# Linear attention fused with two feed-forward layers: when the first layer's weights are converted, and where three mixes stand

## The chip, the cores and the metric

The kernel runs on one core of a Trainium2 chip, as one program. The metric is the time of one execution on the device, in microseconds (us); of several runs the median counts. The core has TensorE (PE: matmuls and transposes, with its weight loads PEld), VectorE (DVE), ScalarE (ACT), GpSimd (POOL) and SyncE (SP, which here only issues DMAs). Matmuls read SBUF and write PSUM, which has eight banks.

## The reference

Three layers run one after the other on 8 batches, 8 heads, 576 positions and heads of 64, in fp32:

```python
def phi(x):                                  # q, k: (8, 8, 576, 64); w_phi: (64, 128)
    proj = x @ w_phi
    proj = proj - np.max(np.abs(proj), axis=-1, keepdims=True)
    return np.concatenate([np.exp(proj), np.exp(-proj)], axis=-1)
q_p, k_p = phi(q), phi(k)
kv = einsum('bhsf,bhsd->bhfd', k_p, v);  z = k_p.sum(axis=2)
x = (q_p @ kv) / (q_p @ z + 1e-6)            # heads laid side by side: (8, 576, 512)

x_prev = x shifted by one position
xk = mu_k * x + (1 - mu_k) * x_prev;  xr = mu_r * x + (1 - mu_r) * x_prev
k = relu(xk @ w_k)                           # w_k: 512 x 1024
x = sigmoid(xr @ w_r) * ((k * k) @ w_v)      # w_r: 512 x 512, w_v: 1024 x 512

h = relu(x @ w_in)                           # w_in: 512 x 1024
c = conv over 3 positions of h, per feature
out = (h * sigmoid(c)) @ w_out               # w_out: 1024 x 512
```

The weights of both feed-forward layers arrive in fp64 and are made fp32 on the chip.

## The kernel before

**Attention, by pairs.** The eight heads of a batch are four pairs, 32 pairs in all, and `block(Pi)` is the TensorE work of one. In the block of pair k TensorE does, from pair 5 on, in this order: the transposes `px` of the result of pair k-1 (whose copy `xT` ScalarE makes); the transposes `pt` of the query features of pair k, which ScalarE turns into `qf` by four Exp, two for each head; the products `pk` of pair k+2 and `pq` of pair k+1, whose maxima `mx` and differences `t` VectorE makes; the sums `pkv` of pair k+1; and the results `pn` of pair k, which VectorE divides into `xn`. In the blocks of pairs 1 to 4 (up to `MS`) `px` stands behind `pk`. `p` is the short last piece of `pk`, and `pr` that of `px` and `pt`. PSUM banks come from two pools: `psa` with five (`pt`, `px`, `pr`, `pkv`, `pn` and some of `pk`), and `psm` with three (the rest of `pk`, `pq`, and all of the layer below). A tile that takes over a bank waits for those who read the bank before: `pkv` takes the one of the second `pt`, and so waits for the last of its `qf`.

**The first feed-forward layer, by units.** `moe(u)` handles half a batch, 16 units in all, in 20 steps: eight `psk` (xk by w_k; ScalarE's Relu makes `kf`, and the square, its cast `kh` and the rest `kl` follow), and twice two `psr` (xr by w_r; Tanh makes `sg`) and two `psv` (by w_v; VectorE makes `x`, which goes to DRAM), each `psv` with two steps. `mix(u, j)` makes xk (j = 0) or xr (j = 1) of unit u from the four `xT` of its batch: for unit 0 four pairs of a ScalarE `mh` and a VectorE `mh`, from unit 1 on four ScalarE `xf` with four VectorE ones, two casts `mh` and two differences `ml`. From unit 1 on a product is three matmuls of hi and lo halves (`mm3`); unit 0 uses the unsplit fp32 weights, one matmul each.

**What runs beside what.** The program counts fifteen places n in a pair; `block(Pi)` is issued at the first. `feed(Pi)` issues the next steps of the units: `SR[Pi]` of them in pairs 4 to 7, ten a pair from pair 8 (`SLOW`). Pairs 0 to 3 have none. `mix(u, 1)` of an odd unit gives the `xT` of a batch back; six are held (`XT`), and a block that would need one more makes the units run on first (`while done[0] * NP <= Pi - 1 - XT`). TensorE's order is the order of the program. The order of the other engines is the scheduler's, which may move an instruction ahead of others.

**The weights' parts.** wk, wr and wv are 20 parts of 512 columns, 512 KB of fp64 each. A part (`step`) is in three pieces: SyncE loads it into one of three buffers `raw`; ScalarE makes `h` from it (the Abs, an ACTIVATE h<-raw); VectorE does two TENSOR_SCALAR and two SCALAR_TENSOR_TENSOR on `h`, after which SyncE writes the 256 KB of `h` to its place in `wkl`, `wrh` or `wvl` and `ready` counts one up. `tick()` issues the load of a new part, the Abs of the one before (through `pre()`, which can also stand earlier) and the end of the one two back. The load of a part needs the buffer of the part three earlier, so VectorE must be through with that. `split` later makes a part's two halves: a cast on ScalarE (`wkh` and the like) and a subtraction on VectorE. From pair 10 on the weights of the last layer pass through in the same way, in smaller pieces `hc` and `whl`.

**When a part is asked for.** The blocks of pairs -1 to 6 call `tick()` twice each. `extras` ticks at the places that `WAT` lists: twice in pair 4, three times in pair 5, four times in pair 6. And `want(n)` ticks at a step of unit 0 or 1 until `n + AHEAD` parts are ready. `split` may run as soon as a part is whole: unit 0 calls it around its `psv`, unit 1 after each `psk` and `psr`.

After the last pair the rest of the units and the second feed-forward layer run (`psh`, `pso`); the change doesn't touch them.

Of the kernel before, what the change touches and what calls it, by code (L numbers as in the profile page):

```python
# [25 lines left out]

NS = 15

MS, SLOW, SR = 4, 8, {4: 6, 5: 6, 6: 7, 7: 9}

WAT = {4: (4, 10), 5: (3, 7, 11), 6: (3, 5, 7, 9)}
DS0 = 10
AHEAD = 2
HS = S // 2
V1 = D + 1

# [6 lines left out]
def fused_kernel(ctx: ExitStack, tc: tile.TileContext, qk, va, wphi, ones2, mu, wk, wv, wr, win, wout, cw, out):  # L43
# [113 lines left out]
    with ExitStack() as p1:  # L157
# [29 lines left out]

        def split(n=None):

            while n is None or cleft[0] < n:  # L190
                if half:
                    hs, ls = half.pop()
                    V.behind("tensor_tensor", ls, f(ls), f(hs), ALU.subtract)
                    cleft[0] += 1
                if whole and (n is None or cleft[0] < n):
                    half.append(whole.pop(0))
                    A.behind("copy", half[0][0], f(half[0][1]))
                if n is None or not half:
                    return
# [3 lines left out]
        def pre():  # L203

            if under and under[0][1] == 2 and not under[0][2]:
                next(under[0][0])
                under[0][2] = True

        def tick():
            pre()  # L210
            new = [wsteps.pop(0), 0, False] if wsteps else None
            if new:
                next(new[0])
            if under and under[0][1] == 2:
                next(under.pop(0)[0], None)
            if new:
                under.append(new)
            for x in under:
                x[1] += 1

        wsteps = [step(wk, wkh, wkl, o) for o in range(0, 4096, 512)]
        for h in range(2):
            for w in ((wr, wrh, wrl), (wv, wvh, wvl)):
                n = w[1].shape[1] // 2
# [163 lines left out]
        def block(Pi):  # L388

            nq, nk = Pi + 1 < B * NP, Pi + 2 < B * NP  # L390
            if 0 <= Pi < B * NP - 3:
                load(Pi + 3)
            if Pi >= 0:
                if Pi > MS:
                    x = column(Pi - 1)
                qf, t1 = turn(Pi)
                pr = psa.tile([P, 512], F32, tag="at", name="pr")
                if Pi > MS:
                    copies = column_end(*x, pr)
                turn_end(qf, t1, pr)  # L400
                if Pi > MS:
                    copies()
            pre()
            if nk:
                tk = front(Pi + 2)
            if -1 <= Pi < 7:
                tick()
            if 1 <= Pi <= MS:
                x = column(Pi - 1)
                column_end(*x, psm.tile([P, 512], F32, tag="mm", name="pr"))()  # L410
            if nq:
                ts[Pi + 1] += centre4(rows4(Pi + 1, 0, "pq"), "tq")
                del xk[Pi + 1]
                sums4(Pi + 1)
            if Pi >= 0:
                results(Pi, qf)
            pre()
            if nk:
                features(Pi + 2, tk)
                if Pi + 2 > 1:  # L420
                    load_v(Pi + 2)
            if -1 <= Pi < 7:
                tick()

        def attention(Pi):
# [30 lines left out]
        def mix_next(u, j):  # L456
            if (u, j) in mixed:
                return True
            if u >= 2 * B or any((u // 2, c) not in xT for c in range(KC)):
                return False  # L460
            mixed[u, j] = mix(u, j)
            if j and u % 2:
                done[0] = u // 2 + 1
            return True

        done = [0]

        def want(n):

            while ready[0] < min(n + AHEAD, 20):  # L470
                tick()
            due[0] += 1

        due = [0]
        needs = [*range(1, 9), 9, 10, 12, 14, 15, 16, 18, 20]

        def moe(u):
            b, hf = divmod(u, 2)

            def mm(ps, wh, wl, xh, xl, first, last):  # L480
                if u:
                    mm3(ps, wh, wl, xh, xl, first, last)
                else:
                    T.matmul(ps, f(wl), xh, start=first, stop=last)

            def need(n):
                want(n)
                if u:
                    split(n)

            def soon():
                if u == 0 and due[0] < len(needs) and ready[0] < min(needs[due[0]] + AHEAD, 20):
                    pre()
            o = hf * HS
            for j in range(2):
                while not mix_next(u, j):
                    yield
            xh, xl = mixed.pop((u, 0))
            k2 = []
            for fp in range(FC // 2):  # L500
                kf = tmps.tile([P, 2, HS], F32, tag="tmp", name="kf")
                for j in range(2):
                    ps = psm.tile([P, 512], F32, tag="mm", name="psk")[:, :HS]
                    fc = 2 * fp + j
                    need(fc + 1)
                    for c in range(KC):
                        w = slice(fc * DM + c * P, fc * DM + c * P + P)
                        mm(ps, wkh[:, w], wkl[:, w], xh[:, c], xl[:, c], c == 0, c == KC - 1)
                    A.activation(kf[:, j], ps, AF.Relu)
                    soon()  # L510
                    if u == 1:
                        split()
                    yield
                if u == 0:
                    kh = main.tile([P, 2, HS], F32, tag="kh", bufs=4, name="kh")
                    A.square(kh, kf)
                    k2.append((kh, kh))
                    continue
                if u == 1:
                    A.square(kf, kf)  # L520
                else:
                    V.tensor_tensor(kf, kf, kf, ALU.mult)
                kh = main.tile([P, 2, HS], F32R, tag="kh", bufs=4, name="kh")
                kl = main.tile([P, 2, HS], F32R, tag="kl", bufs=4, name="kl")
                A.copy(kh, kf)
                V.tensor_tensor(kl, kf, f(kh), ALU.subtract)
                k2.append((kh, kl))
            rh, rl = mixed.pop((u, 1))
            for mp in range(2):
                sg = main.tile([P, 2, HS], F32, tag="sg", bufs=1, name="sg")  # L530
                for j in range(2):
                    ps = psm.tile([P, 512], F32, tag="mm", name="psr")[:, :HS]
                    mc = 2 * mp + j
                    need(9 + 6 * mp + j)
                    for c in range(KC):
                        w = slice(mc * DM + c * P, mc * DM + c * P + P)
                        mm(ps, wrh[:, w], wrl[:, w], rh[:, c], rl[:, c], c == 0, c == KC - 1)
                    A.activation(sg[:, j], ps, AF.Tanh, scale=0.5)
                    soon()
                    if u == 1:  # L540
                        split()
                    yield
                mix_next(u + 1, mp)
                x2 = tmps.tile([P, 2, HS], F32, tag="tmp", name="x2")
                for j in range(2):
                    ps = psm.tile([P, 512], F32, tag="mm", name="psv")[:, :HS]
                    mc = 2 * mp + j
                    need(12 + 6 * mp + 2 * j)
                    for kc in range(FC):
                        w = slice(mc * DFF + kc * P, mc * DFF + kc * P + P)  # L550
                        kh, kl = k2[kc // 2]
                        mm(ps, wvh[:, w], wvl[:, w], kh[:, kc % 2], kl[:, kc % 2], kc == 0, kc == FC - 1)
                    if u < 2:
                        split()
                    soon()
                    yield
                    if u < 2:
                        split()
                    V.scalar_tensor_tensor(x2[:, j], sg[:, j], 1.0, ps, ALU.add, ALU.mult)
                    yield  # L560
                (SY if u else G).dma_start(x2s[b][:, 2 * mp:2 * mp + 2, o:o + HS], x2)
# [12 lines left out]
        load_v(1)  # L574

        def extras(Pi, n):
            if n in WAT.get(Pi, ()):
                tick()
            if n + 1 in WAT.get(Pi, ()):
                pre()  # L580
            if Pi == 7 and n == 14:
                taps()
            if Pi >= DS0 and dsteps and n in (3, 11):
                dsteps[0] = dsteps[0][0](), dsteps[0][1]
            if Pi >= DS0 and dsteps and n in (4, 12):
                raw, step = dsteps.pop(0)
                step(raw)
# [177 lines left out]
```

## Time and profile before

| | |
|---|---|
| median of 3 runs | 1226.19 us (1225.79 to 1226.19) |
| the profiled execution | 1225.83 us, of which its span 1224.0 us |
| PE busy | 1202.0 us (98%), 11920 matmuls |
| PEld busy | 1135.5 us (93%) |
| DVE busy | 762.1 us (62%), 1584 instructions |
| ACT busy | 696.7 us (57%), 1644 instructions |
| POOL busy | 86.3 us (7%) |
| DMA | 100.81 MB, mean 82 GB/s; 223 to 196 GB/s in the first four of the 40 slices, 59 to 80 in the next four |
| chain that ended last | PE 90%, DVE 5%, ACT 2%, issue 1%, DMA 1% |

The span is what the profiler's records cover; the time of the execution is 1.8 us more. Shares of busy time are means over the whole. The first 130 us, in which the weights of the first layer come in and the first pairs run, are where the change is made; after them TensorE is busy in every slice.

### The profile page before, as it was taken

How to read it: one execution, taken by the hardware profiler on the slowest of the kernel's cores; microseconds unless marked ns; L12 is line 12 of the kernel's file. 1: busy time of each engine (PE TensorE's matmuls, PEld its weight loads, DVE VectorE, ACT ScalarE, POOL GpSimd, SP SyncE). 2: the span in 40 equal slices, each digit the busy share in tenths (PEclk: the TensorE clock that was granted, in tenths of full speed). 3: DMA queues.
4: the chain of work that ended last, by engine and by line, in shares of the span. 5: the costliest groups of instructions: out<-in, count | busy, mean ns of one | idle time of the engine just before them, and what ended most of it. 6: DMA issues, size and time to landing. Idle time of an engine off the chain costs nothing.

```text
span 1224.0 us, 29034 instructions
## 1 busy us (share of the span) xinstructions
PE 1202.0 (98%) x11920; PEld 1135.5 (93%) x11920; DVE 762.1 (62%) x1584; ACT 696.7 (57%) x1644; POOL 86.3 (7%) x213
## 2 busy tenths in 40 slices
PE   7899999999999999999999999999999999999998
PEld 6787999999999999999999999998889888888887
DVE  7989676576675765766656534426555754466555
ACT  6777765566565655665555533325654655455554
POOL 1000001111111111111000000000000000000000
PEclk9999999999999999999999999999999999999999
DMA  6665121223232322332110004050122101210220
GB/s 223 221 218 196 59 80 59 86 93 120 89 93 76 117 83 86 93 121 71 50 42 23 11 21 158 20 188 19 44 63 63 43 21 62 63 53 11 63 62 32
DMA packets 56532, 100.81 MB, mean 82 GB/s; under 512 B 10320, under 2 KB 38608, under 8 KB 56400
## 3 DMA queue, kind: packets, MB, share of 16 engines
q1 hardware_dynamic: 40272, 61.65, 14.8%
q0 software_dynamic: 6768, 27.69, 7.4%
q10 hardware_dynamic: 9360, 9.61, 2.8%
q8 instruction: 94, 1.54, 0.5%
q14 instruction: 38, 0.31, 0.1%
HBM read 66.42 MB, written 27.26 MB: 77 GB/s over the span
## 4 chain that ended last, share of the span: by engine, by line
PE 90%; DVE 5%; ACT 2%; issue 1%; DMA 1%; SPq 0%; ACTq 0%; DVEq 0%
PE psh L150 5%; PE psh L152 5%; PE psh L151 5%; PE psv L150 5%; PE pkv L318 5%; PE psv L151 5%; PE psk L151 5%; PE psv L152 5%; PE psk L152 5%; PE psk L150 5%; PE pso L150 5%; PE pso L151 5%; PE pso L152 5%; PE pn L371 4%; PE psr L150 3%; PE psr L151 3%
## 5 line engine op out<-in xcount | busy, mean ns | idle before, releaser
L58 DVE SCALAR_TENSOR_TENSOR ct<-h,cw,ct 128x460 f32<-128x460 f32 (+2 forms) x160 | 111.4, 696 | 84.6 <-ACT ct L58 83.5
L150 PE MATMUL psv<-kh,wvl 128*128 128x288 f32 x480 | 142.2, 297 | 0.0
L151 PE MATMUL psv<-kl,wvh 128*128 128x288 f32 x480 | 141.9, 296 | 0.0
L151 PE MATMUL psk<-ml,wkh 128*128 128x288 f32 x480 | 141.7, 295 | 0.0
L152 PE MATMUL psk<-mh,wkh 128*128 128x288 f32 x480 | 141.4, 295 | 0.0
L152 PE MATMUL psv<-kh,wvh 128*128 128x288 f32 x480 | 141.1, 294 | 0.0
L150 PE MATMUL psk<-mh,wkl 128*128 128x288 f32 x480 | 140.9, 294 | 0.0
L152 PE MATMUL psh<-xh,wih 128*128 128x462 f32 (+1 forms) x320 | 118.9, 372 | 0.0
L151 PE MATMUL psh<-xl,wih 128*128 128x462 f32 (+1 forms) x320 | 118.8, 372 | 0.0
L151 PE MATMUL pso<-gl,woh 128*128 128x460 f32 (+1 forms) x320 | 117.9, 370 | 0.0
L152 PE MATMUL pso<-gh,woh 128*128 128x460 f32 (+1 forms) x320 | 117.7, 370 | 0.0
L58 ACT ACTIVATE kf<-psk 128x288 f32<-128x288 f32 x128 | 52.2, 408 | 111.5 <-PE psk L152 105.6
L150 PE MATMUL psh<-xh,wil 128*128 128x462 f32 (+1 forms) x320 | 107.3, 372 | 0.0
L58 ACT ACTIVATE h<-psh 128x462 f32<-128x462 f32 (+3 forms) x128 | 47.8, 409 | 76.8 <-PE psh L152 75.6
L150 PEld LDWEIGHTS psv<-kh,wvl 128*128 128x128 f32 x480 | 90.3, 188 | 0.8
L151 PEld LDWEIGHTS psv<-kl,wvh 128*128 128x128 f32 x480 | 90.4, 188 | 0.0
L150 PEld LDWEIGHTS psk<-mh,wkl 128*128 128x128 f32 x480 | 90.2, 188 | 0.1
L151 PEld LDWEIGHTS psk<-ml,wkh 128*128 128x128 f32 x480 | 90.2, 188 | 0.0
L152 PEld LDWEIGHTS psv<-kh,wvh 128*128 128x128 f32 x480 | 90.2, 188 | 0.0
L152 PEld LDWEIGHTS psk<-mh,wkh 128*128 128x128 f32 x480 | 90.2, 188 | 0.0
L58 ACT ACTIVATE kp<-t 128x512 f32<-128x512 f32 x128 | 70.3, 618 | 34.6 <-PE pkv L318 28.9
L58 DVE SCALAR_TENSOR_TENSOR x<-sg,psv 128x288 f32<-128x288 f32 x64 | 29.0, 454 | 97.5 <-PE psv L152 91.4
(108 smaller groups left out, 2822.7 us busy)
## 6 DMA issues: line engine op xcount, KB each, us to landing
rqk<-qk POOLq DMA_DIRECT2D x29, 576.0 KB, 4.8
va<-va POOLq DMA_DIRECT2D x30, 325.0 KB, 4.8
x2s<-x SPq DMA_DIRECT2D x30, 288.0 KB, 2.3
raw<-wk SPq DMA_DIRECT2D x8, 512.0 KB, 5.4
raw<-wv SPq DMA_DIRECT2D x8, 512.0 KB, 4.0
raw<-win SPq DMA_DIRECT2D x16, 256.0 KB, 2.9
raw<-wout SPq DMA_DIRECT2D x16, 256.0 KB, 2.9
x2r<-x2s ACTq DMA_DIRECT2D x16, 231.0 KB, 2.6
```

The costliest lines, as they stand in the source:

```text
L58: x = op(*a, **k)
L150: T.matmul(ps, wl, xh, start=first, stop=False)
L151: T.matmul(ps, wh, xl, start=False, stop=False)
L152: T.matmul(ps, wh, xh, start=False, stop=last)
L318: T.matmul(o[r:r + 64], k_[:, r:r + 64], v_, start=(i == 0), stop=(i == len(prods) - 1))
L371: T.matmul(pn[b_][64 * r:64 * r + 64, j], qf[h_][:, c, o:o + 64], kv[:, c, h_], start=(j == 0 and c == 0), stop=(j == 4 - b_ and c == 1))
```

## The change

- **Parts.** In the blocks of pairs -1 to 4 the first `tick()` stays, and the second only in pair -1's. So pairs 0 to 3 issue one part instead of two, pair 4 one, and the blocks of pairs 5 and 6 none. The table `WAT`, its ticks in `extras` and `AHEAD` go. Instead every step of unit 0 that needs a part ticks until `ready` has reached the larger of what it needs and `PRE + RATE * (at + 1)`, with `at` the number of the step: one part a step, six ahead. `soon()` issues the Abs of a part that the next step will ask for.
- **Splits.** A `split` without a number does nothing until all 20 parts are ready.
- **Mixes.** Units 0 and 1 start with `mix(u, 0)` alone. `mix(0, 1)` is called after the fourth `psk` of unit 0, `mix(1, 1)` after the second of unit 1 (before: in unit 0, between its last `psr` and `psv`), and `mix(1, 0)` after the last `psr` of unit 0 (before: after its second `psr`).
- **Steps.** `SR[7]` goes from 9 to 6.

```diff
-MS, SLOW, SR = 4, 8, {4: 6, 5: 6, 6: 7, 7: 9}
-WAT = {4: (4, 10), 5: (3, 7, 11), 6: (3, 5, 7, 9)}
-AHEAD = 2
+MS, SLOW, SR = 4, 8, {4: 6, 5: 6, 6: 7, 7: 6}
+PRE, RATE = 6, 1.0
@@ split
         def split(n=None):
+            if n is None and ready[0] < 20:
+                return
@@ block
-            if -1 <= Pi < 7:
+            if -1 <= Pi <= MS:
                 tick()
...
-            if -1 <= Pi < 7:
+            if Pi == -1:
                 tick()
@@ want
-        def want(n):
-            while ready[0] < min(n + AHEAD, 20):
-                tick()
-            due[0] += 1
-        due = [0]
-        needs = [*range(1, 9), 9, 10, 12, 14, 15, 16, 18, 20]
+        needs = [*zip([*range(11), 12, 14, 15, 16, 18], [*range(1, 11), 12, 14, 15, 16, 18, 20])]
+        def goal():
+            at, n = needs[0]
+            return min(20, max(n, int(PRE + RATE * (at + 1))))
+        def want():
+            while ready[0] < goal():
+                tick()
+            needs.pop(0)
@@ moe
             def need(n):
-                want(n)
                 if u:
                     split(n)
+                else:
+                    want()
             def soon():
-                if u == 0 and due[0] < len(needs) and ready[0] < min(needs[due[0]] + AHEAD, 20):
+                if u == 0 and needs and ready[0] < goal():
                     pre()
-            for j in range(2):
+            for j in range(2 if u > 1 else 1):
                 while not mix_next(u, j):
                     yield
...
+                if fp == 1 - u:
+                    mix_next(u, 1)
...
-                mix_next(u + 1, mp)
+                if u:
+                    mix_next(u + 1, mp)
+                elif mp:
+                    mix_next(1, 0)
@@ extras
-            if n in WAT.get(Pi, ()):
-                tick()
-            if n + 1 in WAT.get(Pi, ()):
-                pre()
```

How this moves instructions shows at three places. The first is VectorE at the start of pair 3's block: the last division `xn` of pair 2, and what stands up to the differences `t` of `pk`. Before:

```order
L58 TENSOR_SCALAR xn<-pn,rd 128x128
L58 TENSOR_SCALAR h<-h 128x512
L58 TENSOR_REDUCE mx<-p_876 128x1
L58 TENSOR_REDUCE mx<-p_877 128x1
L58 TENSOR_SCALAR h<-h 128x512
L58 TENSOR_TENSOR t<-p_876,mx 128x128
L58 TENSOR_TENSOR t<-p_877,mx 128x128
L58 SCALAR_TENSOR_TENSOR h<-raw,h 128x512
L58 TENSOR_REDUCE mx<-pk 128x4 x2
L58 SCALAR_TENSOR_TENSOR h<-raw,h 128x512
```

After:

```order
L57 TENSOR_SCALAR xn<-pn,rd 128x128
L57 TENSOR_REDUCE mx<-p_849 128x1
L57 TENSOR_REDUCE mx<-p_850 128x1
L57 TENSOR_TENSOR t<-p_849,mx 128x128
L57 TENSOR_TENSOR t<-p_850,mx 128x128
L57 TENSOR_REDUCE mx<-pk 128x4 x2
L57 TENSOR_TENSOR t<-pk,mx 128x512 x2
L57 TENSOR_SCALAR h<-h 128x512
```

The four instructions of one part, which stood among the small steps and around the reduction of `pk`, are gone from there; the pair's remaining part follows behind `t`.

The second is ScalarE at the end of pair 4, among the `kf` of unit 0, and at the start of pair 5's block, which begins with the copy `xT`. Before:

```order
L58 ACTIVATE kf<-psk 128x288
L58 ACTIVATE h<-raw 128x512
L58 ACTIVATE kf<-psk 128x288
L58 ACTIVATE kh<-kf 128x576
L58 ACTIVATE kf<-psk 128x288 x2
L58 COPY xT<-px 128x512
L58 ACTIVATE kh<-kf 128x576
L58 ACTIVATE qf<-pt 128x512 x4
```

After:

```order
L57 ACTIVATE kf<-psk 128x288 x2
L57 ACTIVATE kh<-kf 128x576
L57 ACTIVATE h<-raw 128x512
L57 ACTIVATE kf<-psk 128x288
L57 ACTIVATE h<-raw 128x512
L57 ACTIVATE kf<-psk 128x288
L57 COPY xT<-px 128x512
L57 ACTIVATE kh<-kf 128x576
L57 ACTIVATE qf<-pt 128x512 x3
L57 ACTIVATE h<-raw 128x512
L57 ACTIVATE qf<-pt 128x512
```

An Abs now stands ahead of each of the last two `kf` of pair 4 (the latter part 10's), and part 11's ahead of the fourth `qf`.

The third is ScalarE at pair 12's block, one of the later pairs, with the last `kf` of pair 11 ahead of it. Before:

```order
L58 ACTIVATE kf<-psk 128x288 x2
L58 ACTIVATE hc<-raw 128x256
L58 COPY xT<-px 128x512
L58 ACTIVATE qf<-pt 128x512 x4
L58 CAST kh<-kf 128x576
L58 ACTIVATE qf<-pr 128x64 x4
L58 COPY xT<-pr 64x64 x2
L58 CAST whl<-hc 128x256
L58 ACTIVATE xf<-xT,mu_76 128x288 x4
```

After:

```order
L57 ACTIVATE kf<-psk 128x288
L57 CAST kh<-kf 128x576
L57 ACTIVATE sg<-psr 128x288
L57 COPY xT<-px 128x512
L57 ACTIVATE qf<-pt 128x512 x2
L57 CAST whl<-hc 128x256
L57 ACTIVATE xf<-xT,mu_76 128x288 x2
L57 ACTIVATE qf<-pt 128x512 x2
L57 ACTIVATE qf<-pr 128x64 x4
```

The cast `whl` and two of the `xf`, which stood behind the block's `qf`, stand between its second and third, and a unit's step more is done ahead of the block (the `sg` is the first of its `psr`).

## Rows read from the trace of the kernel before

**Rows 1.** Windows: stretch, length, busy us (count) by engine, clock, DMA share, GB/s

```profile
47.20:58.88 11.68, 9.49 (x196) 8.44 (x196) 11.61 (x29) 9.24 (x25) 1.07 (x2) 1.00 0.66 213
69.53:135.98 66.45, 65.09 (x749) 55.01 (x745) 57.82 (x127) 43.84 (x107) 5.10 (x12) 1.00 0.56 189
135.98:148.79 12.81, 12.81 (x100) 12.81 (x97) 7.13 (x14) 11.43 (x25) 0.00 (x0) 1.00 0.05 18
200.00:500.00 300.00, 300.00 (x3941) 295.45 (x3941) 204.01 (x471) 182.66 (x474) 45.62 (x62) 1.00 0.31 95
```

**Rows 2.** Waits of TensorE, whole span: who for whom, total us, times, longest

```profile
PE psv L484 <- DVE x L58: 0.7, 1, 0.7
...
PE pn L371 <- DVE t L58: 0.7, 1, 0.7
```

**Rows 3.** Order of time, TensorE: start, us, operation, form, count, [idle before <-releaser]

```profile
50.33 1.25 PE L261 MATMUL pk<-wp,rqk 64*128 64x128 f32 x16 [1.24 <-DVE xn L58]
51.51 0.66 PE L330 MATMUL px<-ident,xn 128*128 128x128 f32 x4
...
69.53 11.91 PE L484 MATMUL psk<-mh,wkl 128*128 128x288 f32 x48
```

**Rows 4.** Order of time, VectorE in pair 3's block

```profile
50.35 0.42 DVE L58 TENSOR_SCALAR h<-h 128x512 f32<-128x512 f32 x1
50.69 0.48 DVE L58 TENSOR_REDUCE mx<-p 128x1 f32<-128x128 f32 x2
...
51.81 0.69 DVE L58 SCALAR_TENSOR_TENSOR h<-raw,h 128x512 uint32<-128x512 uint32 x1
52.41 1.29 DVE L58 TENSOR_REDUCE mx<-pk 128x4 f32<-128x512 f32 x2
```

**Rows 5.** Order of time, TensorE and VectorE in pair 5's block

```profile
84.23 1.06 PE L261 MATMUL pq<-wp,rqk 64*128 64x128 f32 x16
84.42 1.29 DVE L58 TENSOR_REDUCE mx<-pk 128x4 f32<-128x512 f32 x2
```

**Rows 6.** Order of time, SyncE's DMA issues and ScalarE in pair 4

```profile
72.45 0.47 SPq L184 DMA_DIRECT2D wrh<-h  x1
73.02 0.90 SPq L174 DMA_DIRECT2D raw<-wv  x1
...
77.05 0.68 ACT L58 ACTIVATE h<-raw 128x512 f32<-128x512 f32 x1 [0.97 <-DMA raw<-wv]
```

**Rows 7.** Tile raw, 60 to 81 us: its loads, issue to landing

```profile
DMA to landing us min/median/max: 3.7/4.7/5.6
```

**Rows 8.** Order of time, TensorE and ScalarE in pair 8's block

```profile
148.79 0.60 PE L330 MATMUL px<-ident,xn 128*128 128x128 f32 x4
...
153.71 2.09 PE L318 MATMUL pkv<-va,kp 128*64 128x65 f32 x64
...
151.01 0.57 ACT L58 COPY xT<-px 128x512 f32<-128x512 f32 x1
```

**Rows 9.** Order of time, TensorE and ScalarE in pair 10's block

```profile
198.71 0.60 PE L330 MATMUL px<-ident,xn 128*128 128x128 f32 x4
...
202.64 1.56 PE L318 MATMUL pkv<-va,kp 128*64 128x65 f32 x46
...
200.84 0.68 ACT L58 CAST kh<-kf 128x576 fp32r<-128x576 f32 x1
201.41 1.11 ACT L58 ACTIVATE qf<-pt 128x512 f32<-128x512 f32 x2
```

**Rows 10.** Order of time, ScalarE behind pair 12's `qf`

```profile
252.33 0.41 ACT L58 CAST whl<-hc 128x256 fp32r<-128x256 f32 x1
252.64 1.87 ACT L58 ACTIVATE xf<-xT,mu 128x288 f32<-128x288 f32 x4
```

**Rows 11.** Order of time, ScalarE and TensorE in pair 26's block

```profile
592.91 2.05 ACT L58 ACTIVATE qf<-pt 128x512 f32<-128x512 f32 x4
594.04 1.16 PE L261 MATMUL pq<-wp,rqk 64*128 64x128 f32 x16 [0.67 <-ACT qf L58]
```

## The prediction

> **What bounds the kernel now.** I read first the busy time by stretch, then TensorE's waits, then the order of time around each wait. From 200 to 500 us TensorE is busy for all of 300.00 us while VectorE has 204 and ScalarE 183 [rows 1]: there TensorE sets the time, and whatever it is made to wait comes on top in full. The first pairs are another regime: pair 3's block takes 11.68 us, VectorE works 11.61 of them and TensorE 9.49 [rows 1]; it is VectorE's. Between them, from 69.53 to 135.98 us, both are nearly full (65.09 and 57.82 of 66.45), with waits of 0.7 for t and 0.7 for x [rows 1, 2]. So the change can gain in pairs 0 to 4 and has to pay where it puts the work. All matmuls stay, so only waits count.
>
> **Two parts a pair become one (pairs 0 to 3).** A part costs VectorE two TENSOR_SCALAR, each 0.34 from its start to the next instruction's (50.35 to 50.69), and two SCALAR_TENSOR_TENSOR at 0.60 (51.81 to 52.41): 1.88 us [rows 4]. A pair loses one part. Not all of it is gained, since the part's steps filled VectorE's wait for pk. The matmuls pk start at 50.33, when xn is done, and take 1.18 until px at 51.51 [rows 3]; VectorE's reduction stands 0.19 behind their end (84.42 behind 84.23) [rows 5], so it can start at 51.70. Without the fillers VectorE is free at 50.35 plus twice 0.40 for the four small steps, 51.15: it idles 0.55. Net 1.33 a pair. Pairs 1 to 3 stand ahead of the first psk, so that moves from 69.53 [rows 3] to 65.5: **4.0 gained** so far. Nothing else is late there: ScalarE loses an Abs too.
>
> **The parts arrive in pairs 4 to 6.** Five parts more (9.4 us) have to go through VectorE there, where it had 66.45 - 57.82 = 8.6 idle [rows 1]; one split of 0.6 leaves. That alone fills it. What I expect to hurt first is ScalarE, whose queue now holds the Abs of the coming parts between the kf and ahead of the copy xT, so that a late load holds everything behind it. There are three raw buffers: part 10's load waits until part 7 is done, and part 7's until part 4 is. In the trace the write that marks the end of pair 4's part leaves at 72.45, the next load 0.57 later, and it has landed at 77.05, 4.03 after its issue [rows 6]. Now, with 4 x 1.33 less: part 4 done at 67.1, load 67.7, landed 71.7, Abs 0.6, VectorE 1.88, so part 7 is done at 74.3; load 74.9, landed 78.9. Behind it on ScalarE stand Abs (0.6), the sixth kf (0.35) and the copy xT, at 79.9. TensorE's px comes after six psk (11.91 with the last one's tail [rows 3], 11.8 to the next start) at 77.3. In pair 8 of the trace, the one block where that copy was late, pkv followed 2.70 behind the copy's start (151.01 to 153.71) [rows 8]; with kh and part 11's Abs put among the qf (1.2 more) pkv is at 83.8 instead of px + 3.93 = 81.2 [rows 9]. **Pair 5 waits 2.6.** By the same steps (part 11 done 89.2, load of 14 landed 93.8, done 96.4, load of 17 landed 101.0, Abs) pair 6's copy starts at 101.6 to 102.9 against a px at 99.9 to 100.5: pkv 0.5 to 1.2 late, **0.9** taken.
>
> The Trainium skill's page "DMA: Bandwidth & Descriptors" (Anatomy of one DMA) gives 2.0 us and bytes over 436 GB/s, an estimate of 3.2 us for 512 KB; by it both loads together come 1.7 earlier and the sum below would be 1228.8. The rows speak against it: 3.7 is the shortest load of 60 to 81 us, the median is 4.7 [rows 7]. The same page (Issuing engines are not separate DMA queues) says that transfers of all issuers interleave on the same 16 engines, which bears on the third rival.
>
> **The mixes.** Of mix (0,1) nothing moves: the order shows its steps still in pairs 1 to 4, so 0. Mix (1,1) goes from pair 6 to unit 1's first steps, where ScalarE already had 11.43 of 12.81 us [rows 1], and three psk now stand ahead of pair 7. Behind the first kf ScalarE has three kf (0.31), three casts of weights (0.51), four xf (0.43), one mh and one square (0.57 each): 5.3 us, while TensorE reaches px 3.2 behind the first psk. The copy starts 2.4 behind px, another mh of 0.57 stands ahead of the qf, and pkv is at px + 2.4 + 0.57 + 2.70 = px + 5.7: **pair 7 waits 1.8**, where it waited for nothing. Pair 8: pkv was 4.92 behind px (148.79 to 153.71) [rows 8], so 1.0 late; now sg, a square and an mh stand around the copy, by the same count px + 5.2: 1.2 late.
>
> The waits of pairs 5 to 8 are then 2.6 + 0.9 + 1.8 + 1.2 = 6.5; before they were 0.7 + 0.7 + 1.0 = 2.4 [rows 2, 8]. With the 4.0 gained the stage is at **+0.1**: the relief is given back. Splits that come later cost nothing: ScalarE's and VectorE's share of them is in the counts above.
>
> **Every second pair from 12 to 26.** With pair 7's rate at 6 and four forced steps the units run one step later against the pairs, and the scheduler puts other ScalarE work into the blocks. In pair 12 and seven like it the cast whl and two xf now stand between the second and third qf; pkv takes over the bank that the fourth qf reads, so it waits for that. The nearest row is pair 10, with a kh of 0.57 in that place (200.84 to 201.41): its qf end at 201.41 + 0.96 = 202.37, pkv starts at 202.64 [rows 9]. From the end of a qf to the matmul that waits for it is 0.17 (592.91 + 0.96 to 594.04) [rows 11]; so pair 10 had 0.10 to spare. Now 0.31 + 2 x 0.43 = 1.17 [rows 10] stands where 0.57 stood: 0.60 more, and the copy starts about 0.02 later, so pkv waits **0.52**. TensorE has no slack there [rows 1]: 8 x 0.52 = 4.2. Pairs 10 and 28 are changed alike by smaller pieces, 0.35 each by the same count; the 0.67 in pair 26 [rows 11] goes: **+4.2** together. Bounds: without the 0.17 it is 0.35 a pair, and 0.67 is the largest wait of this kind in the trace, so +2.1 to +5.4.
>
> **Sum.** The profiled execution: 1225.83 + 0.1 + 4.2 = 1230.1. The median of the runs is 0.36 above that execution: **1230.5**, 0.35% slower.
>
> **Rivals.**
> *The relief survives.* ScalarE is never the last to release TensorE in pairs 5, 6 and the later ones: then 4.0 and 2.4 are gained, pairs 7 and 8 cost 3.0, and the time is 1222.8. It decides at ScalarE's copies: part 10's load would have to be in at 77 rather than 78.9, and the fourth qf in pair 12 half a microsecond sooner. For it: VectorE, not ScalarE, was the engine with no idle time. Against: two loads in a chain, none shorter than 3.7.
> *Even.* The stage gives the relief back, but in pairs 12 to 26 pkv does not wait: 1226.3. It needs the fourth qf released at px + 3.93; the count has it at px + 4.45. For it: kh in the same place cost nothing in pair 10. That the change does not do what it says in one piece (mix (0,1)) is in all of these.
> *The loads collide.* 768 KB a part, read and written back, at one in some 2.4 us. If both loads of the chain take 5.6, the longest there [rows 7], and not 4.03, pair 5 waits 3.1 longer: 1233.6, and more if pair 6's do too. For it: the DMA share is already 0.56 there [rows 1] with fewer parts.
>
> **How the numbers follow.** Forecast 0.5, even 0.2, relief 0.15, collision 0.15. The forecast's own range is 1227.9 to 1232.5, by the bounds of +2.1 to +5.4 and of 0.5 to 1.2 in pair 6. About 0.2%, 2.5 us, is what a measurement of this kernel can tell from no change. Slower by more: 0.46 of the forecast's 0.5 and the collision, 0.61; within: 0.04 and the even case, 0.24; faster: 0.15. The range 1224.5 to 1234.0 leaves out most of the relief (below it) and the worse half of the collision (above).
>
> **What would show it.** Right: first psk near 65.5; pair 2's and 3's blocks 10.35 apart; in pair 5 TensorE waits for xT or qf, with ScalarE's Abs waiting for raw just before; in pairs 12, 14 and so on to 26 pkv waits for qf by about half a microsecond. Wrong: blocks of 9.8 (the pk wait is not there), pair 5 of 8.5, or no wait of TensorE for ScalarE from pair 12 on. The prediction falls if psv waits for a part's write, which I put at nothing, or if blocks that I did not count wait.

## The result: 0.55% slower

The changed kernel takes 1233.49 us (median of 6 runs, 1230.43 to 1234.03), the kernel before, beside it, 1225.97 (1225.27 to 1226.19): a ratio of 1.0055, with a 95% interval of 1.0043 to 1.0067. The forecast was 1230.5, in a range of 1224.5 to 1234.0. The sign came out as forecast, and so did the waits that make it; the terms of pairs 5 and 6 were too small by 3.7 us together, since the parts that they hang on came later than worked out. The profiled execution took 1233.2, with a span of 1231.4 (before: 1225.83 and 1224.0). From the page of the profile after:

```profile
span 1231.4 us, 29055 instructions
PE 1205.6 (98%) x11920; PEld 1138.4 (92%) x11920; DVE 768.4 (62%) x1584; ACT 697.5 (57%) x1644; POOL 82.5 (7%) x213
PE 87%; DVE 6%; ACT 5%; DMA 1%; issue 1%; ACTq 0%; SPq 0%; DVEq 0%
```

The matmuls are the same 11920. What is new is in the chain that ended last (the third line): ScalarE has 5% of it, 2% before. TensorE's waits over the whole span, in the manner of [rows 2], name it: the copy xT ahead of pk, and qf ahead of pkv eleven times.

```profile
PE pk L262 <- ACT xT L57: 5.4, 3, 2.6
PE pkv L319 <- ACT qf L57: 4.7, 11, 0.5
...
PE pk L262 <- DVE xn L57: 4.1, 4, 1.2
```

Where the 7.4 us of span went is seen by holding the length of each pair's block on TensorE (from px to the first step of a unit behind pn) against before:

| | before | after | difference | forecast |
|---|---|---|---|---|
| first psk starts at | 69.53 | 65.44 | -4.1 | -4.0 |
| pair 5 | 8.50 | 12.67 | +4.2 | +2.6 |
| pair 6, with the wait of psv behind it | 9.37 + 0.70 | 11.65 | +1.6 | -0.5 |
| pair 7 | 8.49 | 10.22 | +1.7 | +1.8 |
| pair 8 | 9.48 | 9.61 | +0.1 | +0.2 |
| pairs 9 to 28 | 20 x 8.50 + 1.0 | 20 x 8.50 + 5.08 | +4.1 | +4.2 |
| sum | | | +7.6 | +4.3 |

(The forecast's pair 6 is 0.9 less 0.7 and 0.7.) From pair 29 on the blocks are alike. TensorE's last matmul ends 7.8 later, and what follows it is 0.4 shorter. In pair 12's block the order of time has ScalarE as the order of instructions said, with the cast and two xf between the second and third qf, and TensorE's pkv waiting for the fourth:

```profile
254.60 1.10 ACT L57 ACTIVATE qf<-pt 128x512 f32<-128x512 f32 x2
255.57 0.43 ACT L57 CAST whl<-hc 128x256 fp32r<-128x256 f32 x1
255.86 0.99 ACT L57 ACTIVATE xf<-xT,mu 128x288 f32<-128x288 f32 x2
256.73 1.10 ACT L57 ACTIVATE qf<-pt 128x512 f32<-128x512 f32 x2
...
257.88 2.09 PE L319 MATMUL pkv<-va,kp 128*64 128x65 f32 x64 [0.46 <-ACT qf L57]
```

Such blocks are 9.03 for 8.50: 0.53, where the forecast, from the 0.10 that pair 10 had to spare [rows 9], had 0.52.

Pairs 5 and 6 are where the forecast fell short. In pair 5, ScalarE first (the Abs of parts 9, 10 and 11, the copy and the fourth qf), then TensorE:

```profile
77.15 0.67 ACT L57 ACTIVATE h<-raw 128x512 f32<-128x512 f32 x1 [1.22 <-DMA raw<-wr]
77.72 0.40 ACT L57 ACTIVATE kf<-psk 128x288 f32<-128x288 f32 x1
80.40 0.66 ACT L57 ACTIVATE h<-raw 128x512 f32<-128x512 f32 x1 [2.27 <-DVE h L57]
80.96 0.40 ACT L57 ACTIVATE kf<-psk 128x288 f32<-128x288 f32 x1
81.25 0.58 ACT L57 COPY xT<-px 128x512 f32<-128x512 f32 x1
...
83.74 0.70 ACT L57 ACTIVATE h<-raw 128x512 f32<-128x512 f32 x1
84.29 0.63 ACT L57 ACTIVATE qf<-pt 128x512 f32<-128x512 f32 x1
...
79.24 0.38 PE L262 MATMUL pk<-wp,rqk 64*128 64x128 f32 x2
81.89 1.85 PE L262 MATMUL pk<-wp,rqk 64*128 64x128 f32 x13 [2.27 <-ACT xT L57]
...
85.29 2.09 PE L319 MATMUL pkv<-va,kp 128*64 128x65 f32 x64
```

Part 10's Abs stands in the queue ahead of the last kf and the copy, as forecast, and it starts at 80.40, where 78.9 was forecast. Its load was issued at 75.62 and took 4.7. (The profile puts the wait down to VectorE, which had finished part 9 at 80.20; in the program this Abs waits for two DMAs alone, its load and an older write of h.) The copy comes at 81.25, and the second of pk's two banks, which px had, is free only then: TensorE stands still in pk already, after two of its sixteen matmuls.

Behind this wait the clock falls. The windows of the stretch (columns as in [rows 1]) have TensorE still from 79.60 to 81.89, and then at half its clock:

```profile
79.60:81.89 2.29, 0.02 (x1) 0.00 (x1) 1.36 (x3) 1.49 (x4) 0.00 (x0) 0.91 0.90 322
81.89:83.90 2.01, 2.01 (x17) 2.01 (x19) 1.98 (x7) 2.01 (x5) 0.00 (x0) 0.50 0.94 282
83.90:85.30 1.40, 1.40 (x19) 1.28 (x16) 1.40 (x5) 1.40 (x7) 0.00 (x0) 0.64 0.54 199
...
104.00:106.62 2.62, 0.04 (x2) 0.01 (x1) 2.58 (x7) 2.62 (x7) 0.00 (x0) 1.00 0.83 265
106.62:109.00 2.38, 2.38 (x40) 2.25 (x42) 2.38 (x8) 2.38 (x9) 0.00 (x0) 1.00 0.30 111
```

A granted clock of 0.50 is 1.2 GHz, the lower of its two levels; with the mean of 0.64 in the third row, TensorE worked at it for some 3.0 us behind the wait. That costs little here, since pkv has to wait for the fourth qf in any case. The kernel of e3 (below) is the same up to pair 7, and in its trace the clock is 1.00 throughout pair 5:

```profile
79.91 0.58 ACT L57 COPY xT<-px 128x512 f32<-128x512 f32 x1
...
80.53 1.16 PE L262 MATMUL pk<-wp,rqk 64*128 64x128 f32 x14 [0.91 <-ACT xT L57]
82.09 1.16 PE L262 MATMUL pq<-wp,rqk 64*128 64x128 f32 x16 [0.40 <-ACT qf L57]
83.63 2.09 PE L319 MATMUL pkv<-va,kp 128*64 128x65 f32 x64 [0.38 <-ACT qf L57]
```

From the copy's start to pkv it is 3.72 there and 4.04 here, so the clock makes 0.3 of the 4.2. What else sets the two traces apart is when the copy comes: 79.91 there, where part 10's load was issued at 75.02 and took 3.9, and 81.25 here. The block of e3 is 11.00, 2.5 over 8.50.

In pair 6 the copy comes at 106.00, behind the Abs of parts 16 and 17 and four xf of mix (1,0):

```profile
103.17 0.67 ACT L57 ACTIVATE h<-raw 128x512 f32<-128x512 f32 x1 [2.75 <-DMA raw<-wv]
103.74 1.79 ACT L57 ACTIVATE xf<-xT,mu 128x288 f32<-128x288 f32 x4
105.45 0.65 ACT L57 ACTIVATE h<-raw 128x512 f32<-128x512 f32 x1
106.00 0.56 ACT L57 COPY xT<-px 128x512 f32<-128x512 f32 x1
...
99.53 0.54 SPq L173 DMA_DIRECT2D raw<-wv  x1
DMA to landing us min/median/max: 5.5/5.5/5.5
```

The last two lines are part 17's load: issued at 99.53, in at 105.0. TensorE stood still for 2.58 in this block, longer than in pair 5, and its clock stayed at 1.00 (the last two of the windows). Where the clock fell in pair 6 (e1, e3 and e5 to e8), the stretch from the copy to the end of the block is 8.7 to 8.8; without a fall (here, e4 and e9) it is 7.2. So a fall costs some 1.5 there, and 0.3 in pair 5 here.

The six runs of the changed kernel differ with the clock too: the one whose mean granted clock was 1.000 took 1230.43, the two with 0.999 took 1231.0 and 1233.2, the three with 0.996 to 0.998 took 1233.77 to 1234.03. How much of that is the clock, and how much the late loads that go before a fall, these runs don't show. The kernel before, which has no wait over 0.7 there [rows 2], varies by 0.9.

### The profile page after: what moved, and what is told of

Same layout as the page of the kernel before. It is cut to its first block, busy times and chain, and to the rows that moved or that the text cites. A ratio compares the mean times of both kernels' runs of the same rounds, so it can differ in the third digit from the quotient of the medians.

```text
span 1231.4 us, 29055 instructions
## 1 busy us (share of the span) xinstructions
PE 1205.6 (98%) x11920; PEld 1138.4 (92%) x11920; DVE 768.4 (62%) x1584; ACT 697.5 (57%) x1644; POOL 82.5 (7%) x213
## 3 DMA queue, kind: packets, MB, share of 16 engines
q10 hardware_dynamic: 9360, 9.61, 2.8%
## 4 chain that ended last, share of the span: by engine, by line
PE 87%; DVE 6%; ACT 5%; DMA 1%; issue 1%; ACTq 0%; SPq 0%; DVEq 0%
PE psh L149 5%; PE psh L151 5%; PE psh L150 5%; PE pkv L319 5%; PE psv L150 5%; PE psv L151 5%; PE psv L149 5%; PE psk L149 5%; PE pso L149 5%; PE psk L150 5%; PE psk L151 5%; PE pso L150 5%; PE pso L151 5%; PE pn L372 4%; PE psr L149 3%; PE psr L150 2%
## 5 line engine op out<-in xcount | busy, mean ns | idle before, releaser
L149 PE MATMUL pso<-gh,wol 128*128 128x460 f32 (+1 forms) x320 | 88.0, 371 | 0.3 <-ACT gh L57 0.3
```

Of the source, the lines that this page charges most:

```text
L149: T.matmul(ps, wl, xh, start=first, stop=False)
```

## The experiments

Times of the experiments are medians beside runs of the kernel before on the same chip: 1225.74 for e1 to e4, 1225.82 for e5 to e8, 1225.64 for e9 to e12.

**The two halves of the change, apart (e1, e2).** e1 is the changed kernel with the mixes and SR[7] of before:

```diff
-MS, SLOW, SR = 4, 8, {4: 6, 5: 6, 6: 7, 7: 6}
+MS, SLOW, SR = 4, 8, {4: 6, 5: 6, 6: 7, 7: 9}
...
-            for j in range(2 if u > 1 else 1):
+            for j in range(2):
...
-                if fp == 1 - u:
-                    mix_next(u, 1)
...
-                if u:
-                    mix_next(u + 1, mp)
-                elif mp:
-                    mix_next(1, 0)
+                mix_next(u + 1, mp)
```

> The changed kernel with the mixes where they stood before and 9 steps again in pair 7; the parts stay as changed. Theory (three separate prices: the parts gain 4.1 in pairs 1 to 3 and cost 4.2 + 2.3 - 0.7 in pairs 5 and 6 through ScalarE's copy xT; mixes and steps cost 1.7 in pair 7 and 4.1 in pairs 10 to 28): blocks of pairs 5 and 6 stay long (12.7 and 11.6), pair 7 is back at 8.5 and every second pair from 12 on at 8.5; 1226.0 - 4.1 + 4.2 + 2.3 - 0.7 = 1227.7 (1225.5 if TensorE's clock does not fall in pair 5). Rival (the mixes, not the parts, hold up pairs 5 and 6): 1222.

e2 is the kernel before with these edits the other way round.

> The kernel before with only the three mixes moved and 6 steps in pair 7; the parts and splits stay as before. Theory: first psk at 69.5, pairs 5 and 6 as before (8.5 and 9.4), pair 7's block 1.7 longer, pairs 10, 12 to 26 and 28 about 0.5 longer each: 1226.0 + 1.7 + 0.1 + 4.1 = 1231.9. Rival (the mixes hurt only where the parts are late): 1226.

e1 took 1227.67 (ratio 1.0016, 1.0007 to 1.0025): pairs 5 and 6 at 11.06 and 13.04, pair 7 at 8.50, pairs 9 to 28 at 1.03 over 20 x 8.50, as before. e2 took 1230.50 (1.0040, 1.0028 to 1.0053): pair 5 at 8.50, pair 7 at 10.23, pairs 9 to 28 at 5.08 over. Of the 1.4 that it is under the expected time, 1.0 is that pair 6 and the psv behind it wait less than before (8.50 and 0.54 for 9.37 and 0.70). So the two halves come near the whole: 1.9 for the parts, 4.8 for mixes and steps, 6.7 of 7.5, and each cost shows in the pairs that it was put down to. The rival that the mixes hold up pairs 5 and 6 is out.

**One step (e3).** In the changed kernel, pair 7 gets 5 steps:

```diff
-MS, SLOW, SR = 4, 8, {4: 6, 5: 6, 6: 7, 7: 6}
+MS, SLOW, SR = 4, 8, {4: 6, 5: 6, 6: 7, 7: 5}
```

> The changed kernel with 5 steps in pair 7 for 6, which puts the units back by one step against the pairs. Theory (the waits of pkv for qf in every second pair from 10 on come from that one step alone): they go, blocks of 8.5 from pair 9 on with pair 26's 9.46 back; 1233.5 - 4.1 = 1229.4, pairs 1 to 8 unchanged. Rival (they come from where mixes and splits stand): 1233.5.

It took 1228.25 (1.0017, 1.0008 to 1.0026). Pairs 9 to 28 are back at 1.02 over 20 x 8.50, so the 4.1 there come from the one step by which the units ran on against the pairs, and from nothing else in the change. The other 1.1 is not located: pairs 5 and 6 take 11.00 and 13.65 in this trace, 12.67 and 11.65 in the change's, and the eleven runs go from 1225.83 to 1230.78.

**Parts four ahead instead of six (e4).**

```diff
-PRE, RATE = 6, 1.0
+PRE, RATE = 4, 1.0
```

> The changed kernel with PRE 4 for 6: the last Abs ahead of pair 5's copy xT is that of part 9, not 10, and ahead of pair 6's that of part 15, not 17. Theory (the copy stands behind an Abs whose load has not landed): part 9 was in at 77.1, so the copy comes at 78.3, TensorE does not wait in pair 5 (8.5 to 9.2 for 12.67) and its clock does not fall; pair 6 keeps the four xf ahead of the copy and waits 1 to 2; psk and psr do not wait for parts: 1228 to 1230. Rival (the loads collide, whatever stands in ScalarE's queue): 1233.5 or more, with TensorE waiting for parts.

It took 1235.33 (1.0077, 1.0065 to 1.0090): 1.8 slower than the change, where 3.5 to 5.5 faster was expected. The first half of the theory held: the copy came at 77.97, and pairs 5 and 6 took 9.59 and 9.34. But TensorE now waited for the parts themselves:

```profile
PE psv L489 <- DMA wvl<-h: 3.3, 4, 1.6
PE psr L489 <- DMA wrh<-h: 2.4, 1, 2.4
```

So the wait does not go with the copy's place behind the Abs: taken out of ScalarE's queue, it turns up where a part is needed. (With PRE 4 each part is also asked for two steps later, so a share of it can be of this edit's own making.)

**Half loads, half VectorE work (e5, e9).** e5 loads 256 columns of a part and reads them twice; e9 lets VectorE's four instructions cover 256 columns.

```diff
 # e5
-            SY.dma_start(raw, src[:, o_])
+            SY.dma_start(raw[:, :256], src[:, o:o + 256])
...
-            high, low, hu = raw[:, :, 1], raw[:, :, 0], h.bitcast(U32)
+            high, low = [raw[:, :256, i].unsqueeze(1).to_broadcast([P, 2, 256]) for i in (1, 0)]
...
 # e9, ahead of VectorE's four instructions
+            h, hu, low, high = h[:, :256], hu[:, :256], low[:, :256], high[:, :256]
```

> The changed kernel with loads of half a part (256 columns, 256 KB for 512 KB; the Abs and VectorE's steps keep their size and read those columns twice, so half of the first layer's weights are left out and their values are wrong). Theory (the copy xT of pairs 5 and 6 stands behind an Abs whose load is still under way): loads of 2.5 to 3 for 4.4, the chain of three buffers some 1.5 a part shorter, no wait of ScalarE for raw ahead of these copies: blocks of 8.5 to 9.5 in pairs 5 and 6 for 12.67 and 11.65, TensorE's clock stays; pairs 12 to 26 keep their 9.03; 1227 to 1228. Rival (VectorE, full in pairs 4 to 6, is what holds the parts): both blocks stay over 11 and the time over 1232.

> The changed kernel with whole loads, but VectorE's four instructions of a part on 256 of its 512 columns (half of the first layer's weights stay unconverted, their values are wrong). Theory after e5 (VectorE is the engine that sets when a part is done: 2.25 a part when it does parts one after the other, and with half loads it had no idle left ahead of pair 6's copy): a part takes 1.2, pairs 1 to 3 lose another 0.3 each, pairs 5 and 6 take 8.5 to 9.5 for 12.67 and 11.65; 1225 to 1227. Rival (the loads are the limit, 4.3 each through three buffers): pairs 5 and 6 stay at 11 or more; 1231 or more.

e5: 1230.67 (1.0043, 1.0029 to 1.0057); e9: 1233.42 (1.0069, 1.0053 to 1.0084). Neither theory stands alone. With loads of 2.9 (median) for 4.3, pairs 5 and 6 still took 10.51 and 12.73: VectorE then went from part to part without a gap and was still late. With half of VectorE's work they took 13.67 and 10.59, ScalarE standing for loads of 4.5; in e9 the order also has part 11's Abs, not part 10's, as the last ahead of pair 5's copy. One window per kernel, from pair 1's px to the end of the last part on VectorE, shows both (before, after, e5, e9, in this order, each from its own trace):

```profile
28.16:121.36 93.20, 85.30 (x1276) 73.46 (x1276) 88.59 (x203) 68.63 (x170) 7.56 (x17) 1.00 0.63 211
```

```profile
28.43:123.35 94.92, 87.19 (x1279) 76.00 (x1279) 88.04 (x197) 65.85 (x164) 8.64 (x13) 0.98 0.64 204
```

```profile
27.79:119.82 92.03, 85.71 (x1271) 74.66 (x1271) 88.24 (x197) 65.82 (x164) 8.51 (x13) 0.98 0.49 161
```

```profile
27.43:119.05 91.62, 85.28 (x1266) 74.21 (x1266) 74.88 (x197) 65.64 (x166) 7.23 (x13) 0.98 0.63 208
```

The third figure with a count is VectorE. Its work up to the last part is the same 88 us whichever pairs the parts stand in, and before it had only 4.6 of 93.2 idle. So the last part could end at most 4.6 sooner even if VectorE never stood still: that bounds what moving parts can gain. It is not the only limit. In the changed kernel VectorE stood still for 6.9 of 94.9. In e9, with 13 less for VectorE, the last part ends only 4.3 sooner (119.05 for 123.35), and with half loads 3.5 sooner. And in both the changed kernel and e9 part 17 is in by 105.0 and 102.3, but VectorE takes it up only at 116.91 and 114.50, behind pair 6's own steps. Which limit sets the last part in which order is not shown.

**A part back in pairs 0 and 1 (e6, e7, e8).** All three are e1 with a second tick again, e7 and e8 also with PRE 5:

```diff
             if Pi == -1:      # e6, e7: Pi < 1;  e8: Pi < 2
                 tick()
```

> e1 with a second part in pair 0 again (pair 0's block did not get shorter by losing it: 11.16 before, 11.43 after). The order puts part 11's Abs, not part 10's, ahead of pair 5's copy. Theory: 0 to 0.3 lost in pair 0; pair 5 gains little (the chain of loads is one part ahead, and the copy waits for one part more): 11; pair 6, behind part 16 as in e1, gains one part's 2.3: 10.7; 1225.4. Rival (the position counts, not the part): 1227.7, or more with one part more through VectorE.

> e6 with PRE 5, so that pair 5's copy stands behind part 10 and pair 6's behind part 15, each with its load one part earlier than in e1. Theory: pair 5 8.7 to 9.2, pair 6 9 to 9.5 (four xf still ahead of its copy), psr and psv wait 0 to 2 for parts that come later; pairs from 7 on as in e1: 1224. Rival (what the blocks gain is waited for by psr and psv, as in e4): 1227 or more.

> e7 with a second part in pair 1 as well: 1.4 of the 4.1 given back there, and all loads from pair 4 on one part earlier again. Theory: pairs 5 and 6 8.5 to 9, nothing waits for a part in the steps: 1224 to 1225. If e7 is already free of these waits, this is 1.4 slower than e7.

They took 1228.91, 1228.17 and 1229.83 (1.0027, 1.0021 and 1.0038): all three theories missed, by 3.5, 4.2 and 4.8 or more, and the rivals of e6 and e7 came. In e6 pair 5 took 13.14, with part 11's Abs ahead of its copy. In e7 pair 5 took 8.90 as expected, but pair 6 took 12.39, and psv waited 1.7 for wvl; e8 has the same waits and pays 1.8 more ahead of the first psk (67.91 for 66.12).

**The kernel before with one or two parts fewer (e10, e11).**

```diff
-            if -1 <= Pi < 7:                            # the second tick of a block
+            if -1 <= Pi < 7 and Pi != 3:                # e10
...
+            if -1 <= Pi < 7 and Pi not in (2, 3):       # e11
```

> The kernel before without the second part in pair 3 (nothing else). Theory (a part in pairs 1 to 3 costs 1.46 there and 2.25 of VectorE later, where before has 8.6 idle in pairs 4 to 6): first psk 1.46 earlier; one part fits into the idle time, pairs 5 and 6 lose 0 to 1: 1225.0 (1224.3 to 1226). Rival (each part moved costs TensorE what it gains, or more): 1226 to 1227.

> The kernel before without the second part in pairs 2 and 3 (nothing else). Theory: first psk 2.9 earlier; 4.5 more for VectorE in pairs 4 to 6, of 8.6 idle: waits of 1 to 2 in pairs 5 and 6 or in psr and psv; 1224.5 to 1225.5. Rival (each part moved costs what it gains or more): 1226.5 to 1228.

They took 1227.49 (1.0018, 1.0009 to 1.0027) and 1232.62 (1.0058, 1.0045 to 1.0070): the rival was right, and for two parts the cost was higher than it said. In e10 the part left out shortened no block (px of pair 4's block 11.68 behind that of pair 3's, as before), and the last psv of unit 0 waited for a part's write, and then ran at the lower clock, 5.81 for 4.04:

```profile
120.00 4.15 PE L484 MATMUL psv<-kh,wvl 128*128 128x288 f32 x16 [0.71 <-DVE x L58]
126.18 5.81 PE L484 MATMUL psv<-kh,wvl 128*128 128x288 f32 x16 [2.02 <-DMA wvl<-h]
```

```profile
126.00:129.00 3.00, 2.82 (x6) 2.04 (x7) 2.41 (x5) 0.00 (x0) 0.00 (x0) 0.56 0.70 229
```

The write is that of the part before the last. VectorE worked these two parts into each other, and the first of them was whole only after the third of these four instructions:

```profile
121.79 1.90 DVE L58 SCALAR_TENSOR_TENSOR h<-raw,h 128x512 uint32<-128x512 uint32 x3
123.72 0.47 SPq L184 DMA_DIRECT2D wvl<-h  x1
124.23 0.67 DVE L58 SCALAR_TENSOR_TENSOR h<-raw,h 128x512 uint32<-128x512 uint32 x1
```

In the kernel before these two writes leave SyncE at 118.29 and 121.38, and such writes land 2.3 after their issue (median). The last psv starts at 123.61, and its matmuls on the last part stand 1.9 behind that: 3.0 and 1.8 to spare. In e10 they left 5.4 and 3.6 later. In e11 one pair's block became shorter (10.22, 1.46 less), and psv waited 4.1, pkv 2.4.

Where the last part ends on VectorE, and where unit 0's last psv ends on TensorE, in the orders tried:

| | last part | last psv | | last part | last psv |
|---|---|---|---|---|---|
| before | 121.36 | 127.49 | e4 | 126.49 | 130.71 |
| after | 123.35 | 128.93 | e6 | 123.92 | 131.25 |
| e1 | 121.49 | 128.81 | e7 | 124.31 | 128.75 |
| e2 | 121.46 | 125.78 | e8 | 126.00 | 130.44 |
| e3 | 122.21 | 129.00 | e10, e11 | 124.90, 128.14 | 131.82, 134.25 |

No order with fewer parts in pairs 0 to 3 ends the last part sooner than the kernel before, though the first psk starts up to 5 us sooner. (The traces' first px stands at 27.5 to 28.8; counted from it, e1's last part is 0.3 sooner, those of the others 0.6 to 7.5 later.)

**TensorE kept busy in its wait (e12).**

```diff
+            if Pi in (5, 6):
+                for _ in range(20):
+                    T.transpose(pr[:, 3 * P:], t1[:, 0, 0], ident)
             pre()
             if nk:
                 tk = front(Pi + 2)
```

> The changed kernel with 20 transposes more, of about 0.11 each, in the blocks of pairs 5 and 6 between pr and p, into a part of a PSUM bank that nobody reads: TensorE works through most of its wait for the copy xT. Theory (the granted clock falls to 1.2 GHz in some runs because TensorE stands still there, and that makes up what pair 5 takes beyond its wait): clock 1.00 throughout, pair 5 10.8 for 12.67, pair 6 11.0 for 11.65, 1231 to 1231.5, and runs within 1.5 of each other instead of 3.6. Rival (the clock falls for another reason, or its fall costs nothing): 1233.5 with the same spread, or more where the transposes last longer than the wait.

It took 1244.40 (1.0154, 1.0140 to 1.0168), and is inconclusive: the transposes write the bank that holds pr, so that they waited for its readers themselves, behind the copy xT, instead of filling the wait.

```profile
85.16 4.19 PE L406 MATMUL pr<-ident,t 128*128 128x128 f32 x20 [5.93 <-ACT xT L57]
```

```profile
82.00:84.00 2.00, 0.00 (x0) 0.00 (x0) 0.96 (x3) 2.00 (x5) 0.00 (x0) 0.51 0.90 284
84.00:88.00 4.00, 2.84 (x14) 2.85 (x15) 2.17 (x4) 1.77 (x8) 0.00 (x0) 0.50 0.76 258
```

It shows once more a clock that fell while TensorE stood still, and work behind that ran at it. Whether filling the wait would keep the clock up stays open.

No version beats the kernel before. The nearest by their medians are e10, e1, e7 and e3, 1.9 to 2.5 us slower. The fastest runs of e1 and e3, 1225.55 and 1225.83 at a mean clock of 1.000, are no slower than the kernel before (1224.83 to 1227.02), the slowest of both, at 0.996 and 0.997, 4 to 5 us: part of their cost comes and goes with the clock, or with what goes ahead of its falls.

## Why the prediction held, and where it did not

- **The gain in pairs 0 to 3** was right: first psk at 65.44 for 65.5. The blocks are 10.22 apart, not 10.35, so a pair gained 1.46 for 1.33; the count took pairs 1 to 3 alone, and what lies ahead of them indeed gained nothing (the first px at 28.43, 28.16 before).
- **That it would be given back** was right, and by the queue that was named: ScalarE's Abs ahead of the copy, waiting for its load, in pair 5 and in pair 6.
- **Pair 5's term was mis-sized:** 2.6 forecast, 4.2 measured. The forecast had pkv 2.70 and 1.2 behind a copy at 79.9. In e3's trace, with the same code up to there, just that came: copy at 79.91, pkv 3.72 behind it, block 2.5 longer. In the change's trace the copy came at 81.25, 1.3 later: part 7 was done at 75.0 for 74.3, and part 10's load took 4.7 for 4.0. The clock, for which the prediction had no term (the kernel before shows 1.00 in every window read), added 0.3.
- **Pair 6's term was mis-sized:** 0.9 forecast, 3.2 over 8.50 measured. The step that failed is the chain of parts up to the copy, put at 101.6 to 102.9; it came at 106.00, and pkv 2.69 behind it, as the count said (2.70). The chain ran late link by link: part 11 done at 90.8 for 89.2, the load of 14 in at 95.2 for 93.8, part 14 done at 98.9 for 96.4, the load of 17 in at 105.0 for 101.0. Two sizes in it were too small, VectorE's time for a part (next point; part 14 also had to wait for part 13), and the load of 4.03: part 17's took 5.5. The working also has no line for the four xf of mix (1,0) behind part 16's Abs. In the kernel before they ran behind the first kf after pair 5's block, and the four of mix (1,1) stood ahead of pair 6's copy. But they cost little here: without them part 17's Abs could have started at some 105.1 for 105.45.
- **VectorE's cost of a part was taken too low for its new place.** The 1.88 of [rows 4] is the price between other instructions. Where one part follows the next, each instruction stands behind the one that it depends on, and a part takes 2.25 in the trace after:

```profile
92.11 0.88 DVE L57 TENSOR_SCALAR h<-h 128x512 f32<-128x512 f32 x2
93.02 1.42 DVE L57 SCALAR_TENSOR_TENSOR h<-raw,h 128x512 uint32<-128x512 uint32 x2
94.36 0.88 DVE L57 TENSOR_SCALAR h<-h 128x512 f32<-128x512 f32 x2
```

- **The idle time was read from the wrong window.** The 8.6 us that VectorE had left over [rows 1] ran to 135.98. Up to the end of the last part, at 121.36, it had 4.4, and what stands behind cannot take a part:

```profile
69.53:121.36 51.83, 50.47 (x529) 42.16 (x526) 47.43 (x107) 36.27 (x87) 3.27 (x9) 1.00 0.61 208
```

The prediction saw that the parts would fill VectorE, and it took the relief to be given back. That no other order would keep it either is what e4, e6 to e8, e10 and e11 show for themselves; a proof for every order they are not.

- **Mixes and steps** were right to a few tenths in each of their three places: 1.7 of 1.8 in pair 7, 0.1 of 0.2 in pair 8, 4.1 of 4.2 from pair 9 on. So was mix (0,1) at nothing: in e2 the blocks of pairs 1 to 3 are as long as before.
- **The range held, partly by luck.** The median stands 0.5 under its upper end, and the slowest of the six runs, 1234.03, is above it. The two terms that were too small take up nearly all of it above 1230.5, and loads and clock differ between runs. The forecast's own range was added up wrongly: by its bounds it is 1228.0 to 1232.0, not 1227.9 to 1232.5.
- **The rivals.** Neither the relief nor the even case came: pkv waits in every block that was counted. The time is that of the collision (1233.6), and its mechanism came in part. Of the two loads in pair 5's chain it wanted 5.6 each; they took 4.5 and 4.7, those of pair 6's chain 3.8 and 5.5. On the whole loads were hardly longer: from 60 to 109 us they took 3.6 to 5.8, with a median of 4.3, in the kernel before 3.7 to 6.4, with 4.1. The estimate of 3.2 us for such a load, by the Trainium skill's page "DMA: Bandwidth & Descriptors" (Anatomy of one DMA), was met by none of them. That page gives its fit for DMAs that GpSimd issues; these are issued by SyncE.

## What to carry to other kernels

Before work is moved out of a stretch where an engine is full, sum that engine's work up to the point where the moved work is needed, not up to the end of a handy window. If it is nearly as full all the way (here 88.6 of 93.2), its idle time bounds what the move can gain; none of the nine orders tried here kept a gain. A wait that disappears in one engine's queue after a reordering has to be looked for at the consumer of the late data. What lies behind a wait is not all its price, nor all the clock's: look for the next wait that would have held the engine anyway, as the fourth qf did in pair 5. And when a generator's steps are counted out per block, one step more or less shifts which small instructions fall into which queue in every later block: 0.53 us, eight times over, was half of this change's cost.

## What was not expected of the hardware

- After a wait of 2.3 us TensorE's granted clock was 0.50 for some 3.0 us (pair 5 after), and after one of 2.6 us it stayed at 1.00 (pair 6 after). In e1, e3 and e5 it was pair 5 that kept its clock and pair 6 that fell, to a mean of 0.64 to 0.72 over 2.5 us. What decides is not shown by the rows. A fall cost 1.5 us in pair 6, and 0.3 in pair 5, where TensorE had a second wait to come.
- Four dependent VectorE instructions of 512 columns take 2.25 us one behind the other, and 1.88 of VectorE's time with others between them.
- The same load of 512 KB, with the same code ahead of it, took 3.9 us in one trace and 4.7 in another (part 10 in e3 and after).
